# Three small loads requested from ScalarE's queue instead of GpSimd's, in a fused S4 convolution and linear-attention kernel

## The chip, the cores and the metric

The kernel runs on one core of a Trainium2 chip. The metric is the device time of one execution in microseconds (us). A core has five engines with an instruction queue each: TensorE (PE in the profile; its weight loads are PEld), VectorE (DVE), ScalarE (ACT), GpSimd (POOL) and SyncE (SP), which here only requests transfers. A transfer (DMA) is requested by an instruction in the queue of SyncE, ScalarE or GpSimd and is carried out by 16 DMA engines; the request itself occupies the queue of the engine that makes it (ACTq, SPq in the profile).

## What is computed

One input `A_u` of 2048 positions by 512 channels goes through two branches, which a gate mixes. Cut to what matters:

```
g = sigmoid(sum(x * gate_w))                      # one number per position
# branch a: state-space convolution
K = real(sum_n C * exp(dt * A * l) * dt * B)      # dt = exp(log_dt); 512 channels, 2048 taps, 128 states
a = causal convolution of x with K (reference: FFT of length 4096) + x * Dskip
# branch b: linear attention, 32 heads of 16
q, k, v = x @ wqkv
phi(t)  = [softmax(t @ w_phi), softmax(-(t @ w_phi))]
b = (phi(q) (phi(k)^T v) / (phi(q) sum phi(k))) @ wo
out = g * a + (1 - g) * b
```

The inputs are bfloat16. The three small ones in this case are `w_phi` (32 x 16 x 16, 16 KB), `gate_w` (512 numbers, 1 KB) and `Dskip` (512 numbers, 1 KB).

## The kernel before

The work is a list of small nodes (a few instructions each), with an engine, the data that each reads and writes, and an order. `Plan.add` and `Plan.dma` collect the nodes; `Plan.run` emits them in the order of the constant `ORDER`, two characters a node. Nothing is rescheduled when the program is built: within an engine the instructions stand in the order in which the nodes are emitted. Synchronisation between engines is put in by the framework, from the tiles that instructions read and write.

The stages overlap. First the tables and parameters are made (`prepare`, L197 on): sines and exponentials on ScalarE, their arguments on VectorE, index numbers (iota) on GpSimd. At the same time `wqkv` is loaded transposed and folded with `w_phi` on TensorE (`fold`, L519), which gives the weights of the keys (tile WW) and of the queries (Wqp). Then come keys and values (pk L699, vp L680), the convolution's Fourier stages and kernel generation (kps L182), the queries and the mix.

What stands at the start, queue by queue:

- SyncE asks for the six parameter matrices B_re, A_re, A_im, C_re, B_im, C_im (L216, 128 KB each, in this order), then for the transposed load of `wqkv` (L1506, lands in a part of tile Dtab), five transposed loads of x (L500, tile xT), two writes of a split parameter (L352, tile pz), a sixth xT, the value weights (L1509, tile WW) and sixteen pieces of x (L1496, tile UD).
- ScalarE asks for log_dt twice (L1491 as a column, tile ldc; L1492 spread over all partitions, tile ld), loads an activation table (L65), casts the index columns (L237, tile if), then takes exponentials of ld (L68, tile pt) and ldc (tile dtc), loads the table of sines and goes on with twelve sine and absolute-value instructions.
- GpSimd makes the iotas (L41, L46), asks for the three small loads (L1501 wc, L1502 gw, L1503 Dcol_b), then makes two masks (L468, L470), Wphi (L475, from wc and a mask: `w_phi` laid out block-diagonally), gwr (L488, from gw), some constants, two tiles for selE (L456, L458), Dcol and diagD (L482, L483, from Dcol_b) and a cleared tile (L785).
- TensorE transposes the parameters (psri, L372), and then folds (L519, reads Wphi and Dtab).

How a landing is signalled matters here. Each transfer that SyncE or ScalarE requests gets one of eight semaphores, in turn over both queues in the order of emission. A transfer whose semaphore an earlier one still holds waits, in the queue of the engine that requests it, until that earlier one has landed. Transfers that GpSimd requests have semaphores of their own. In the kernel before, the first eight holders are: 0 ldc, 1 B_re, 2 ld, 3 A_re, 4 A_im, 5 C_re, 6 B_im, 7 C_im; the next are the load of `wqkv` (0) and the xT loads (1 to 5).

The node of the small loads is `wsm` in `prepare`, its body `load_small` in `full_kernel`; `eng` of the node only tells the plan which engine's queue it stands in, and the call in the body decides which engine asks. The nodes that read its data name `wsm` among their keys (`at1` Wphi, `at2` diagD, `at3` gwr).

Of the kernel before, what the change touches and what calls it, by code (L numbers as in the profile page):

```python
# [10 lines left out]
ACT = mybir.ActivationFunctionType  # L11
# [186 lines left out]
def prepare(P, nc, g, evict, psum):  # L198
# [16 lines left out]
    for k, src in g.params:  # L215
        P.dma("par", 0.45, 2.5, lambda k=k, src=src: nc.sync.dma_start(out=g.rawd[k][:], in_=src.rearrange("(g p) n -> p g n", p=128)),  # L216
              rw=("", "r" + k), move=0.9)
    for tg in range(4):
        P.dma("ud", 2.0, 2.0, lambda tg=tg: g.load_ud(tg), rw=("", f"ud{tg}"), move=2.5, cnt=4)
    P.dma("wsm", 1.5, 2.0, lambda: g.load_small(), rw=("", "wsm"), move=0.6, cnt=3, eng="POOL")  # L220
    P.dma("wtr", 0.7, 2.0, lambda: g.load_wqk(), rw=("", "wqk"), move=5.0)
    P.dma("wv", 0.5, 2.0, lambda: g.load_wv(), rw=("", "wv"), move=1.7)

# [117 lines left out]
    for qi, (k, col) in enumerate((("Are", "dtc"), ("Aim", "dt2"))):  # L341
        v, h = 2 * qi, 2 * qi + 1
# [190 lines left out]
def keys_and_spectrum(P, nc, g, psum):  # L533
# [6 lines left out]
    def evict(name, get, deps, **kw):  # L540
        return P.add(("ACT", "DVE"), name, lambda: P.copy(*get()), deps, drop=["psum"], **kw)
    polar, sx, xt, kp = prepare(P, nc, g, evict, psum)

    g.XUn = {}
# [884 lines left out]
def full_kernel(tc, A_u, A_A_re, A_A_im, A_B_re, A_B_im, A_C_re, A_C_im, A_log_dt, A_Dskip,  # L1429
                B_x, B_wqkv, B_w_phi, B_wo, gate_w, out):  # L1430
    nc = tc.nc
# [5 lines left out]
    with ExitStack() as ctx:  # L1437
        g, fc, at = Bag(), Bag(), Bag()
        P = Plan(nc, {"XAu": 1, "UDp": 1, "xst": 3, "Ek": 2, "Zk": 2, "vr": 2, "vb": 2, "acc": 1, "r8": 3, "ax": 1, "nrm": 1, "E": 2, "cs": 4, "A": 1, "R": 2,
                      "KD": 1, "XA0": 1, "XK": 2, "Zr": 2, "XUX": 3, "ln": 8}, {"ps": 2, "p0": 2, "bk": 3, "acc": 1, "pf": 2})  # L1440
# [57 lines left out]

        def load_small():
            with nc.allow_non_contiguous_dma(reason="small"):  # L1500
                nc.gpsimd.dma_start(out=g.wc[:], in_=B_w_phi.rearrange("(m h) e f -> (h e) m f", h=8))  # L1501
                nc.gpsimd.dma_start(out=g.gw[:], in_=gate_w.rearrange("(kt p) -> p kt", p=128))  # L1502
                nc.gpsimd.dma_start(out=g.Dcol_b[:], in_=A_Dskip.rearrange("(kt p) -> p kt", p=128))  # L1503

        def load_wqk():
            nc.sync.dma_start_transpose(out=g.wT, in_=B_wqkv[:, 0:1024])  # L1506
# [17 lines left out]
        def stat_tile():  # L1524
            g.pz = dram.tile([2, 2, 512, 128], BF16, name="pz")
        g.load_ld, g.load_ud, g.load_small, g.load_wqk, g.load_wv, g.load_wo = load_ld, load_ud, load_small, load_wqk, load_wv, load_wo
        g.shift_tmp, g.shift_psum, g.stat_tile = shift_tmp, shift_psum, stat_tile
        g.fc, g.act, g.at, g.xT, g.psP, g.aq, g.persist = fc, act, at, xT, psP, aq, persist
# [101 lines left out]
```

## Time and profile before

| | us |
|---|---|
| median of 3 runs | 255.8 |
| lowest, highest | 254.76, 257.3 |
| the profiled execution's own time | 254.74 |
| its span, first to last instruction | 251.5 |
| VectorE busy | 227.2 |
| ScalarE busy | 215.3 |
| TensorE busy | 197.0 |
| GpSimd busy | 12.5 |

The profile is of one execution. Its times count from the start of the span; the 3.2 us between span and time lie around it. A timeline line gives the start, the duration, the engine, the line in the code, the operation with the tile written and the tiles read, and in brackets how long the engine had been idle before and what released it. A chain line gives start, duration and what the chain of work that ended last was doing then; a releaser is inferred from semaphore events.

### The profile page before, as it was taken

The numbers are of one execution on the slowest core, as the hardware profiler recorded it, in microseconds if no ns is written. First come the engines' busy times: TensorE is split into PE (matmuls) and PEld (weight loads), VectorE is DVE, ScalarE is ACT, GpSimd is POOL, SyncE is SP. The second block draws the span as 40 slices with busy tenths as digits, with TensorE's granted clock in tenths as the row PEclk, the third lists the DMA queues.
The fourth block names the chain that finished last, engine by engine and source line by source line (L and its number), as shares of the span: only waits on it lengthen the run. The fifth ranks groups of instructions, "written<-read, shape, count | busy, mean of one in ns | idle before, by whom it ended". The sixth has DMA issues, their size and how long they took to land.

```text
span 251.5 us, 9945 instructions
## 1 busy us (share of the span) xinstructions
PE 197.0 (78%) x4441; PEld 135.7 (54%) x4464; DVE 227.2 (90%) x306; ACT 215.3 (86%) x297; POOL 12.5 (5%) x24
## 2 busy tenths in 40 slices
PE   0447999999855677976889757999998998998940
PEld 0343356567544442552667535675776686786630
DVE  5899998989999997999999999999999999996341
ACT  2998799999999999999999999998999998663200
POOL 8730000000000000000000000000000000000000
PEclk9999999999599999995899999999999999999985
DMA  5999997100790699204001777214955599999784
GB/s 113 212 181 212 160 208 119 41 3 3 227 264 14 183 280 289 93 13 148 23 3 62 176 253 232 64 44 138 245 169 177 174 279 225 256 218 190 164 114 79
DMA packets 78170, 38.01 MB, mean 151 GB/s; under 512 B 57120, under 2 KB 73136, under 8 KB 78128
## 3 DMA queue, kind: packets, MB, share of 16 engines
q1 hardware_dynamic: 75504, 36.71, 60.1%
q10 hardware_dynamic: 2528, 0.66, 1.7%
q8 instruction: 34, 0.56, 1.0%
q0 software_dynamic: 96, 0.02, 0.1%
q14 instruction: 8, 0.07, 0.1%
HBM read 21.12 MB, written 13.11 MB: 136 GB/s over the span
## 4 chain that ended last, share of the span: by engine, by line
ACT 39%; PE 24%; DVE 17%; DMA 10%; issue 6%; SPq 1%; ACTq 0%; DVEq 0%
ACT cs L68 9%; DMA ZT<-Zd 4%; PE kps L182 4%; ACT L65 3%; ACT XAu L148 3%; PE vp L680 3%; ACT xst L148 3%; DMA WW<-in_B_wqkv_dram 3%; ACT XA L148 3%; ACT E L68 2%; ACT Ek L68 2%; PE psz L1266 2%; DMA ld<-in_A_log_dt_dram 2%; PE psy L824 2%; ACT trg L68 2%
## 5 line engine op out<-in xcount | busy, mean ns | idle before, releaser
L182 PEld LDWEIGHTS <-A 128*32 128x32 bf16 x1600 | 27.8, 161 | 6.4 <-issue 2.8
L182 PE MATMUL kps<-R,A 128*32 128x64 bf16 x1600 | 29.3, 229 | 2.5 <-ACT XA L148 0.8
L68 ACT ACTIVATE cs<-args 128x1024 bf16<-128x1024 f32 x32 | 30.8, 1059 | 0.3 <-PE args L1026 0.2
L1103 DVE TENSOR_TENSOR A<-Ctab,Dtab 128x2048 bf16<-128x2048 bf16 x16 | 19.5, 1218 | 0.7 <-PE kps L182 0.7
L1124 DVE TENSOR_TENSOR R<-E,cs 128x2048 bf16<-128x2048 bf16 x16 | 19.5, 1217 | 0.0
L1108 DVE TENSOR_TENSOR A<-Ctab,Dtab 128x2048 bf16<-128x2048 bf16 x16 | 19.5, 1216 | 0.0
L1120 DVE TENSOR_TENSOR R<-E,cs 128x2048 bf16<-128x2048 bf16 x16 | 19.5, 1216 | 0.0
L148 ACT CAST XK<-psB 128x1024 bf16<-128x1024 f32 (+1 forms) x17 | 16.6, 1005 | 2.4 <-PE psB L195 2.4
L68 ACT ACTIVATE E<-args 128x1024 bf16<-128x1024 f32 x16 | 17.1, 1066 | 1.4 <-PE args L1048 1.4
L68 ACT ACTIVATE Ek<-pk 128x512 bf16<-128x512 f32 x32 | 16.7, 598 | 1.1 <-PE pk L699 0.9
L699 PE MATMUL pk<-WW,xT 128*128 128x512 bf16 x57 | 15.4, 417 | 2.7 <-DVE Wqp L150 1.5
L68 ACT ACTIVATE Eq<-pq 128x512 bf16<-128x512 f32 (+1 forms) x28 | 16.8, 700 | 0.7 <-PE pq L843 0.7
L148 ACT CAST Zr<-psz 128x1024 bf16<-128x1024 f32 x15 | 15.8, 1051 | 1.4 <-PE psz L1266 1.4
L1234 DVE TENSOR_TENSOR t<-XUX,XK 128x2048 bf16<-128x2048 bf16 x14 | 16.8, 1215 | 0.0
L843 PE MATMUL pq<-xT,Wqp 128*128 128x512 bf16 x64 | 16.3, 396 | 0.0
L148 ACT CAST XA<-psA 128x1024 bf16<-128x1024 f32 (+1 forms) x15 | 14.8, 1018 | 1.5 <-DVE XA L150 1.5
L65 ACT ACT_TABLE_LOAD x11 | 14.1, 1283 | 2.1 <-issue 1.9
L1266 PE MATMUL psz<-t,TI 128*128 128x512 bf16 x49 | 14.7, 381 | 1.4 <-ACT xT L148 0.4
L189 PE MATMUL psA<-W,KD 128*64 128x128 bf16 x256 | 10.5, 227 | 5.7 <-ACT KD L148 3.1
L589 PE MATMUL psB<-XAu,TB 64*128 64x128 bf16 x256 | 11.0, 241 | 4.3 <-ACT xst L148 1.9
L726 DVE TENSOR_REDUCE Zk<-Ek 128x64 f32<-128x1024 bf16 x12 | 13.9, 1210 | 0.0
L189 PEld LDWEIGHTS <-KD 128*64 128x64 bf16 x256 | 8.4, 113 | 9.5 <-issue 4.9
(208 smaller groups left out, 475.4 us busy)
## 6 DMA issues: line engine op xcount, KB each, us to landing
XUX<-XUd SPq DMA_DIRECT2D x32, 256.0 KB
XUd<-xst SPq DMA_DIRECT2D x8, 512.0 KB
ax<-apd SPq DMA_DIRECT2D x16, 256.0 KB
Zd<-Zr SPq DMA_DIRECT2D x15, 256.0 KB
ZT<-Zd SPq DMA_DIRECT2D x13, 256.0 KB
UD<-in_A_u_dram SPq DMA_DIRECT2D x16, 128.0 KB
XUd<-xst SPq DMA_DIRECT2D x8, 256.0 KB
out_dram<-xT SPq DMA_DIRECT2D x8, 96.0 KB
```

Source lines behind the costliest of these rows:

```text
L65: return self.nc.scalar.preload_act_table_set(name)
L68: return self.nc.scalar.activation(**kw)
L148: self.nc.scalar.copy(out=o, in_=i)
L182: nc.tensor.matmul(kps[32 * dj:32 * dj + 32, g4, e, :], lhsT=A[:, ka, :, :, d].rearrange("p a b -> p (a b)"), rhs=R[:, kr, d, :], start=(i ...
L189: nc.tensor.matmul(ps[64 * ri:64 * ri + 64], lhsT=lhsT, rhs=fc.W1[:, ri].rearrange("p r d -> p (r d)"), start=True, stop=True, tile_positi ...
L843: nc.tensor.matmul(box.ps[:, m - m0, :] if late else box.ps[:], lhsT=g.Wqp[:, kt, 128 * m:128 * m + 128], rhs=xT[:, 4 * b:4 * b + 4, kt, : ...
L1103: nc.vector.tensor_tensor(out=c.A[:, 0:2].rearrange("p o a b c -> p (o a) b c"), in0=g.C[U // 8][:, 0:2, :, d0 % 256:d0 % 256 + 32].rearra ...
L1108: nc.vector.tensor_tensor(out=c.A[:, 2:4].rearrange("p o a b c -> p (o a) b c"), in0=g.C[U // 8][:, 1:3, :, d0 % 256:d0 % 256 + 32].rearra ...
L1120: nc.vector.tensor_tensor(out=c.R[:, :, :, 32:64], in0=t.E[:, 1].unsqueeze(1).to_broadcast([128, 2, 32, 32]), in1=t.cs[:], op=ALU.mult)
L1124: nc.vector.tensor_tensor(out=c.R[:, :, :, 0:32], in0=t.E[:, 0].unsqueeze(1).to_broadcast([128, 2, 32, 32]), in1=t.cs[:, ::-1, :, ::-1], o ...
L1234: nc.vector.tensor_tensor(out=box.t, in0=Ls[r0 // ns].X[:], in1=box.XK[:].unsqueeze(1).to_broadcast([128, 2, 1024]), op=ALU.mult)
L1266: nc.tensor.matmul(box.ps[:, hb, :], lhsT=fc.TI[:, k].rearrange("p t h a -> p (t h a)"), rhs=box.t[:, k, 512 * hb:512 * hb + 512], start=( ...
```

## The change

The node `wsm` is declared for ScalarE, and `load_small` calls ScalarE's queue:

```diff
-    P.dma("wsm", 1.5, 2.0, lambda: g.load_small(), rw=("", "wsm"), move=0.6, cnt=3, eng="POOL")
+    P.dma("wsm", 1.5, 2.0, lambda: g.load_small(), rw=("", "wsm"), move=0.6, cnt=3, eng="ACT")
...
         def load_small():
             with nc.allow_non_contiguous_dma(reason="small"):
-                nc.gpsimd.dma_start(out=g.wc[:], in_=B_w_phi.rearrange("(m h) e f -> (h e) m f", h=8))
-                nc.gpsimd.dma_start(out=g.gw[:], in_=gate_w.rearrange("(kt p) -> p kt", p=128))
-                nc.gpsimd.dma_start(out=g.Dcol_b[:], in_=A_Dskip.rearrange("(kt p) -> p kt", p=128))
+                nc.scalar.dma_start(out=g.wc[:], in_=B_w_phi.rearrange("(m h) e f -> (h e) m f", h=8))
+                nc.scalar.dma_start(out=g.gw[:], in_=gate_w.rearrange("(kt p) -> p kt", p=128))
+                nc.scalar.dma_start(out=g.Dcol_b[:], in_=A_Dskip.rearrange("(kt p) -> p kt", p=128))
```

`ORDER` is unchanged. In the built program the three requests leave GpSimd's queue (29 rows become 26) and stand in ScalarE's between the cast L237 and the exponential of ld (L68). They now take semaphores of the eight: the instruction order of ScalarE, with what each waits for, is

```
L65   LoadActFuncSet
L237  TensorCopy if<-ii             waits for VectorE
L1501 DMACopy wc<-in_B_w_phi_dram   waits for semaphore 1 (B_re landed)
L1502 DMACopy gw<-in_gate_w_dram    waits for semaphore 3 (A_re landed)
L1503 DMACopy Dcol_b<-in_A_Dskip    waits for semaphore 4 (A_im landed)
L68   Activation pt<-ld             waits for semaphore 2 (ld landed)
L68   Activation dtc<-ldc           waits for semaphore 0 (ldc landed)
```

On SyncE the order is the same, and the semaphores of the later transfers are shifted: the five xT loads wait for 2, 5, 6, 7 and 0 instead of 1 to 5, the two pz writes for 1 and 2 instead of 6 and 7, the sixth xT load for 3 (gw) instead of 0, WW for 4 (Dcol_b) instead of 1. On VectorE and TensorE no instruction moves.

## The prediction

> **What bounds the kernel now.** I read the page's busy shares and chain first, then the chain in order of time for the first 30 us, then the timelines of ScalarE, GpSimd, SyncE and TensorE over that stretch, and last its waits. The page says that no single engine bounds the whole, and that the chain that ended last is mostly engine work:
>
> ```profile
> PE 197.0 (78%) x4441; PEld 135.7 (54%) x4464; DVE 227.2 (90%) x306; ACT 215.3 (86%) x297; POOL 12.5 (5%) x24
> ACT 39%; PE 24%; DVE 17%; DMA 10%; issue 6%; SPq 1%; ACTq 0%; DVEq 0%
> ```
>
> GpSimd is 95% idle, and its last work of any weight ends at 15 us. So the change matters only through the start. There the chain in order of time (start, us, what) reads:
>
> ```profile
> 1.25 5.05 DMA ld<-in_A_log_dt_dram
> 6.30 0.02 issue
> 6.33 0.63 ACT pt L68
> 6.96 0.10 ACT dtc L68
> ...
> 12.84 0.95 ACT tgv L307
> 13.80 0.03 issue
> 13.82 1.71 DVE tgv L286
> ```
>
> The chain starts with ScalarE waiting for the load of log_dt, and then follows ScalarE without a gap to 13.8. Whatever makes ScalarE start later at 6.33 makes the whole start later. What surrounds that point is seen in the timelines (start, us, engine, line, work; in brackets the idle time before it and its releaser). ScalarE and its queue:
>
> ```profile
> 0.73 0.49 ACTq L1491 DMA_DIRECT2D ldc<-in_A_log_dt_dram  x1
> 1.25 0.59 ACTq L1492 DMA_DIRECT2D ld<-in_A_log_dt_dram  x1
> 1.88 1.28 ACT L65 ACT_TABLE_LOAD   x1 [1.88 <-issue]
> 3.17 0.20 ACT L237 CAST if<-ii 128x8 f32<-128x8 int32 x1
> 6.33 0.63 ACT L68 ACTIVATE pt<-ld 128x512 f32<-128x512 bf16 x1 [2.96 <-DMA ld<-in_A_log_dt_dram]
> ```
>
> GpSimd, SyncE and TensorE:
>
> ```profile
> 3.19 0.96 POOL L1501 DMA_DIRECT2D wc<-in_B_w_phi_dram  x1
> 3.44 1.16 SPq L216 DMA_DIRECT2D Cim<-in_A_C_im_dram  x1
> 4.15 0.77 POOL L1502 DMA_DIRECT2D gw<-in_gate_w_dram  x1
> 4.64 6.04 SPq L1506 DMA_TRANSPOSE Dtab<-in_B_wqkv_dram  x1
> 4.90 0.85 POOL L1503 DMA_DIRECT2D Dcol_b<-in_A_Dskip_dram  x1
> 6.73 0.34 PEld L372 LDWEIGHTS <-Are 128*128 128x128 bf16 x4 [6.73 <-DMA Are<-in_A_A_re_dram]
> 7.30 0.34 PEld L372 LDWEIGHTS <-Aim 128*128 128x128 bf16 x4 [0.23 <-DMA Aim<-in_A_A_im_dram]
> 8.41 1.50 POOL L475 TENSOR_TENSOR Wphi<-wc,mask 128x512 bf16<-128x512 bf16 x1 [1.74 <-DMA wc<-in_B_w_phi_dram]
> 13.05 0.77 PEld L519 LDWEIGHTS <-Dtab 128*128 128x128 bf16 x8 [2.76 <-DMA Dtab<-in_B_wqkv_dram]
> 27.23 2.98 PE L680 MATMUL vp<-WW,xT 128*128 128x512 bf16 x13 [0.36 <-DMA WW<-in_B_wqkv_dram]
> ```
>
> Two of the TensorE lines are used as clocks: A_re landed just before 6.73 and A_im just before 7.30, because TensorE stood waiting for them. The last line is the only place near the start where the chain has slack: TensorE had been ready 0.36 us before WW landed.
>
> **The change part by part.**
>
> *Taken from GpSimd.* Three requests, 0.96 + 0.77 + 0.85 = 2.58 us of its queue. Its next work, the masks (5.78 to 6.67), would start about 3.4, but Wphi waits for wc, not for the masks. Gain: 0. Wphi ended at 9.91, and its reader (L519) waited until 13.05 for the transposed Dtab, so even an earlier Wphi buys nothing.
>
> *Added to ScalarE: the requests themselves.* The nearest rows are ScalarE's own requests, 0.32 to 0.59 us (0.49 for ldc, which like gw and Dcol_b is four 2-byte elements on each of 128 partitions). Three are 3 x 0.49 = 1.47 us. ScalarE sits idle for 2.96 us between L237 and L68, so taken alone they would be hidden, and the forecast would be no change.
>
> *Added to ScalarE: waits.* This decides the case, and the diff does not show it. A load from SyncE or ScalarE signals its landing on one of eight semaphores in turn, and the ninth such load waits for the first to land, and so on. GpSimd's loads had semaphores of their own. In the built program of the changed kernel wc waits for B_re's semaphore, gw for A_re's, Dcol_b for A_im's. They stand in ScalarE's order after L237 and ahead of pt (L68). B_re is asked for before A_re, so wc is out by 6.73 at the latest. gw can't be asked for before 6.73, nor Dcol_b before 7.30. Then Dcol_b's request ends at 7.30 + 0.49 = 7.79, and with the 0.04 us that lay between request and next instruction after ld (1.84 to 1.88), pt starts at about 7.83, not 6.33: 1.50 us later. Bounds: with 0.32 us for a request (the shortest on ScalarE, at 241.9) 1.33 us; with 1.16 us each, the request of Cim, which SyncE made just ahead of the transposition, gw runs from 6.73 to 7.89, Dcol_b from 7.93 to 9.09, pt starts at 9.13, 2.80 us later. I take 1.50, since ScalarE's own rows are nearest.
>
> *Who waits behind it.* ScalarE's order from pt on has no gap until 22.9 us, so all of it moves: dtc, the table load, the sines, the second-buffer release for VectorE's tgv at 13.82, then ppx, PE's second L519 group at 16.78 (released by ppx), Wqp and WW, and pk at 22.05. pk ended at 26.87 (27.23 less 0.36) and now ends at 28.37. WW is asked for by SyncE, which waits for nothing of this and lands it near 27.2 as before, so vp starts at 28.37 and not 27.23: the delay is 1.50 - 0.36 = 1.14 us. With the bounds: 0.97 and 2.44.
>
> *SyncE's queue.* The three loads enter the rotation, so SyncE's waits move too: the first xT transposition waits for ld (6.30) instead of B_re, the fifth (issued after 16) for Dtab (13.05), the sixth for gw and WW for Dcol_b (both due before 13). All have landed by then; cost 0. The three loads as small packets: the 512 two-byte packets of ldc took about 8 ns each in the trace's packet records, so 1,536 of them are 1536 x 8 / 16 = 0.77 us on each of the 16 DMA engines, against 96 packets of GpSimd's queue at 2.0% of the first 12 us, 0.24 us. So Dtab and WW may land 0.5 us later: 13.6 and 27.7. Dtab is covered by ppx (16.8), WW by pk's new end of 28.37; without that cover WW's 0.5 would be on the path.
>
> *GpSimd's followers.* If wc lands 5.1 us after a request at 6.73 at worst, Wphi runs from 11.8 to 13.3, 0.3 us past the old start of L519, where TensorE then waits for ppx anyway. gw would land by 7.22 + 5.2 = 12.4, holding gwr and the rest of GpSimd's row up by 2.5 us; its first reader in a hurry is selE at 23.7, made from tiles ready at 12.9. Cost 0.
>
> *Sum.* The profiled execution took 254.7 us (span 251.5 and 3.2 around it): 254.7 + 1.1 = 255.9. It lies 1.1 below the median of the three runs, 255.8, so by the median the forecast is 255.8 + 1.1 = 256.9, say 257.0.
>
> *A rule against the trace.* The Trainium skill, DMA: Bandwidth & Descriptors, "Issuing engines are not separate DMA queues", says that asking from several engines saves only the sequencer's issue time, usually small. By that rule the sum would be 0 and the time 255.8, since 1.47 us fit into the idle 2.96. The rows agree about the issue time, but the rule leaves out what the queue waits for, 7.30 against 6.33.
>
> **The rivals.**
>
> *Slower: the transposition holds ScalarE's requests.* SyncE's L1506 is being issued from 4.64 to 10.68, 6.04 us for one request, and gw and Dcol_b are to go out inside it. If the two queues share what makes descriptors, gw goes out at 10.68, Dcol_b ends at 10.68 + 2 x 0.49 + 0.04 = 11.70, pt starts at 11.74, 5.41 later, and vp 5.05 later: 260.8. For it: Cim, just ahead of L1506, took 1.16 against 0.46 to 0.51 for the five loads before it. Against it: ldc beside Bre (0.49 and 0.46) and at the end ScalarE's output requests at 242 beside SyncE's (0.32 and 0.55) show no queueing. No row has a ScalarE request inside a transposition. It decides once pt starts past 9.25 (6.33 + 0.36 + 1% of 255.8). The Trainium skill, same page, "Queues, rings and completion order", says that SyncE and ScalarE each have a ring on every engine but no descriptor generator of their own, which speaks for this rival; no run here shows it yet.
>
> *Hidden after all.* The 1.1 us at 28 us is taken back later where an engine waits for something that did not move, that is for SyncE's requests: 255.8. For it: SyncE issues from 21.3 to 47 without regard to the start. Against it: from 30 to 60 us the waits name engines and no DMA, and the DMA pieces later in the chain (Zd, ZT after 197) hang on data that moves too.
>
> *Faster: GpSimd's traffic goes.* Its packets took 0.24 us per DMA engine in the first 12 us. If A_im lands earlier by all of that, pt still starts at 7.6, and the time is 256.7. To be faster, pt would have to start before 6.33, and A_im land before 5.8. I see nothing for that.
>
> **How the numbers follow.** Forecast (waits bite, requests are short to moderate): 0.64, at 257.0, its own range 256.8 to 258.3. Transposition rival 0.18 at 260.8. Hidden 0.15 at 255.8. A real gain 0.03. About 1%, 2.6 us, is what a measurement of this kernel can tell from no change (its three runs spread over 2.5). The range reaches from 255.3, the hidden case less a half of that spread's lower side, to 260.0, which leaves out most of the transposition rival. Slower by over 1% (above 258.4): that rival and a little of the forecast's upper end, 0.22. Faster 0.03. Within 1%: 0.75.
>
> **What would show it.** In ScalarE's timeline of the changed kernel: three requests after L237, the first by 6.7, the second not before A_re, the third not before A_im, and pt at about 7.8, right behind the third, where ScalarE's wait for ld was. Request lengths near 0.5 support the forecast; one that lasts until L1506 ends supports the rival. vp should start near 28.4 released by pk and no longer by WW. I am wrong if pt starts near 6.33, if the delay at vp is not about 1.1, or if it is 1.1 there and gone at the end.

## The result, and the profile after

The changed kernel takes 257.66 us (median of 19 runs, 255.21 to 262.45), the kernel before 255.32 beside it (19 runs, 254.22 to 258.25). The ratio is 1.0076, 95% interval 1.0047 to 1.0105: 1.94 us slower, between 1.2 and 2.7. The ratio compares the means of the fast executions, 18 of each kernel, and so differs from the ratio of the medians. The profiled execution took 256.0 us (span 253.4, before 251.5).

The page's busy shares and its shares of the chain, of the changed kernel:

```profile
PE 201.9 (80%) x4464; PEld 136.9 (54%) x4464; DVE 227.2 (90%) x306; ACT 215.6 (85%) x297; POOL 8.8 (3%) x21
PE 31%; ACT 27%; DVE 27%; DMA 7%; issue 7%; SPq 0%; ACTq 0%; DVEq 0%
```

VectorE and ScalarE did the same work in the same time, and GpSimd is 3.7 us less busy, which the end does not show. The difference is where things stand in time. The timeline of the changed kernel, ScalarE's and SyncE's requests with TensorE's weight loads as clocks (start, us, engine, line, work, and in brackets the idle time before it and its releaser):

```profile
3.58 0.38 ACTq L1501 DMA_DIRECT2D wc<-in_B_w_phi_dram  x1
5.78 5.63 SPq L1506 DMA_TRANSPOSE Dtab<-in_B_wqkv_dram  x1
6.54 0.38 ACTq L1502 DMA_DIRECT2D gw<-in_gate_w_dram  x1
6.57 0.34 PEld L372 LDWEIGHTS <-Are 128*128 128x128 bf16 x4 [6.57 <-DMA Are<-in_A_A_re_dram]
7.08 0.41 ACTq L1503 DMA_DIRECT2D Dcol_b<-in_A_Dskip_dram  x1
7.10 0.34 PEld L372 LDWEIGHTS <-Aim 128*128 128x128 bf16 x4 [0.20 <-DMA Aim<-in_A_A_im_dram]
7.54 0.63 ACT L68 ACTIVATE pt<-ld 128x512 f32<-128x512 bf16 x1 [4.17 <-DMA wc<-in_B_w_phi_dram]
```

gw is asked for 0.03 us ahead of TensorE's first use of A_re, Dcol_b 0.02 ahead of its first use of A_im: both fit the landings that TensorE waited for. pt follows the third request's end (7.49) by 0.05. Its bracket names wc, which is wrong: wc was asked for at 3.58, and what pt stands behind is the third request. Nor was ld late: in the packet records of the two traces the last of its 128 packets of 1 KB ended at 5.90 before and at 5.86 here. Two requests went out inside SyncE's L1506 (5.78 to 11.41), in 0.38 and 0.41 us.

From pt the delay goes to VectorE through the table of sines. The changed kernel's timeline of VectorE and GpSimd, and further on two rows of VectorE's that are used as marks below (XAu at 74 us, the last wide product at 243):

```profile
14.23 1.04 POOL L483 TENSOR_TENSOR diagD<-ident,Dcol 128x512 bf16<-128x512 bf16 x1
15.03 1.68 DVE L286 TENSOR_SCALAR tgv<-tgc,one 128x1024 int32<-128x1024 f32 x1 [0.48 <-ACT tgv L307]
15.21 0.95 POOL L785 MEMSET KVbd<- 128x1024 bf16 x1
...
74.25 1.21 DVE L150 CAST XAu<-psA 128x1024 bf16<-128x1024 f32 x1
...
242.88 1.21 DVE L1370 TENSOR_TENSOR xT<-psy,gT 128x1024 bf16<-128x1024 f32 x1
```

The same two marks in the kernel before:

```profile
73.11 1.22 DVE L150 CAST XAu<-psA 128x1024 bf16<-128x1024 f32 x1
...
240.62 1.21 DVE L1370 TENSOR_TENSOR xT<-psy,gT 128x1024 bf16<-128x1024 f32 x1
```

tgv is 15.03 - 13.82 = 1.21 us late, XAu 74.25 - 73.11 = 1.14, the last product 242.88 - 240.62 = 2.26. So there are two questions: is the first 1.1 us what was predicted, for the reason given; and does the second 1.1, behind 75 us, belong to the change?

### The profile page after: what moved, and what is told of

The parts are those of the page before. It is cut to its first block, busy times and chain, and to the rows that moved or that the text cites. A ratio compares the mean times of both kernels' runs of the same rounds, so it can differ in the third digit from the quotient of the medians.

```text
span 253.4 us, 9966 instructions
## 1 busy us (share of the span) xinstructions
PE 201.9 (80%) x4464; PEld 136.9 (54%) x4464; DVE 227.2 (90%) x306; ACT 215.6 (85%) x297; POOL 8.8 (3%) x21
## 4 chain that ended last, share of the span: by engine, by line
PE 31%; ACT 27%; DVE 27%; DMA 7%; issue 7%; SPq 0%; ACTq 0%; DVEq 0%
PE pk L699 6%; ACT cs L68 6%; DMA ZT<-Zd 4%; PE vp L680 4%; PE kps L182 4%; DVE A L1108 3%; DVE A L1103 3%; DVE R L1124 3%; DVE R L1120 3%; DVE t L1234 3%; ACT xst L148 3%; ACT L65 2%; ACT XAu L148 2%; ACT trg L68 2%; PE psA L564 2%
## 5 line engine op out<-in xcount | busy, mean ns | idle before, releaser
L68 ACT ACTIVATE cs<-args 128x1024 bf16<-128x1024 f32 x32 | 30.8, 1063 | 0.3 <-PE args L1026 0.2
L699 PE MATMUL pk<-WW,xT 128*128 128x512 bf16 x64 | 17.2, 421 | 1.5 <-DVE Wqp L150 1.5
L68 ACT ACTIVATE E<-args 128x1024 bf16<-128x1024 f32 x16 | 17.0, 1061 | 1.7 <-PE args L1048 1.5
L68 ACT ACTIVATE Ek<-pk 128x512 bf16<-128x512 f32 x32 | 16.7, 598 | 1.3 <-PE pk L699 1.2
L68 ACT ACTIVATE Eq<-pq 128x512 bf16<-128x512 f32 (+1 forms) x28 | 16.7, 694 | 0.7 <-PE pq L843 0.7
L1266 PE MATMUL psz<-t,TI 128*128 128x512 bf16 x60 | 15.5, 380 | 1.2 <-DVE t L1234 0.7
## 6 DMA issues: line engine op xcount, KB each, us to landing
XUX<-XUd SPq DMA_DIRECT2D x32, 256.0 KB
ax<-apd SPq DMA_DIRECT2D x16, 256.0 KB
Zd<-Zr SPq DMA_DIRECT2D x15, 256.0 KB
ZT<-Zd SPq DMA_DIRECT2D x13, 256.0 KB
XUd<-xst SPq DMA_DIRECT2D x8, 256.0 KB
```

What stands on the lines that cost most here:

```text
L68: return self.nc.scalar.activation(**kw)
L699: nc.tensor.matmul(box.ps[:], lhsT=xT[:, st, kt, :], rhs=g.WW[:, kt, :], start=(kt == 0), stop=(kt == 3))
```

## The experiments

The theory on trial: the requests cost nothing; the landings that they wait for on ScalarE hold pt up. Rivals: the requests on ScalarE's queue cost by themselves; the relief of GpSimd changes something. Each kernel's ratio is to the kernel before, timed beside it.

**1. One wait without any move (e1_wait_aim).** The kernel before, with a read of one column of A_im put ahead of pt:

```diff
-    S("p_e", lambda: act(out=Tt(4)[:], in_=g.ld_b[:], func=ACT.Exp), r="act ldb tmp", w="t4")
+    def p_e():
+        w = g.up.tile([128, 1], BF16, name="w_")
+        nc.scalar.copy(out=w[:], in_=g.rawd["Aim"][:, 3, 127:128])
+        act(out=Tt(4)[:], in_=g.ld_b[:], func=ACT.Exp)
+    S("p_e", p_e, r="act ldb tmp", w="t4")
```

> The kernel before, its three loads left on GpSimd, with one added ScalarE instruction ahead of pt (L68): a copy of one column of A_im, whose value nobody uses, so that ScalarE waits for A_im there and asks for nothing. Theory (the wait for the landings is what costs): pt starts near 7.5 instead of 6.33, vp near 28.1, and the time is 0.8 to 1.9 us above the kernel before, about as the changed kernel. Rival (the requests themselves, or their small packets, cost the time): within 0.3 us of before, since none is moved.

Measured: 256.30 us, ratio 1.0038 (1.0004 to 1.0072), so +0.97. ScalarE's timeline:

```profile
6.90 0.19 ACT L257 COPY w__185<-Aim 128x1 bf16<-128x1 bf16 x1 [3.53 <-DMA Aim<-in_A_A_im_dram]
7.00 0.62 ACT L68 ACTIVATE pt<-ld 128x512 f32<-128x512 bf16 x1
```

A wait for A_im alone makes the kernel slower, with all three requests still on GpSimd. pt is 0.67 late here and 1.21 in the changed kernel. The interval is 0.1 to 1.8 us, so the time alone only just speaks against the rival's 0.3.

**2. A later wait (e2_wait_cim).** The same with C_im, the last parameter to land.

> As the run with the wait for A_im, but ScalarE's added copy reads C_im, which landed at 9.0 in the trace of before: a longer dose of the same wait. Theory: pt starts near 9.2, 2.9 later; vp 2.5 later; the time 2.5 us above before if a delay at the start is carried to the end one to one, 3.5 or more if a later start also costs more in the later stages. Rival (later waits on SyncE's queue take a delay up): less than 1.5 us.

Measured: 258.09 us, ratio 1.011 (1.0068 to 1.0151), +2.8. The copy stood until 9.39, pt started at 9.49. pt is 3.16 behind the profile of before, VectorE's XAu only 2.21 (75.32): the missing 0.9 is that tgv took 0.81 us here in place of 1.71. That was not expected, and experiments 7 to 10 follow it up. The time fits the 2.5 us that were expected (the interval is 1.7 to 3.9) and rules out the rival's 1.5 or less; it does not tell 2.5 from 3.5.

**3. The requests behind pt (e3_late).** The changed kernel with the node of the small loads moved in `ORDER` behind pt, dtc and the table load:

```diff
-              "0W0y0B0K0h0i2U030M1f2C2D2E0L1e0l0f1I2I0C2F2G0R2L2M060N0X15...
+              "0W0B0K0h0i2U030M1f2C2D2E0L1e0l0f1I2I0C2F2G0R2L2M060N0y0X15...
```

> The changed kernel with the three requests moved back in ScalarE's queue, behind pt, dtc and the second table load. Their semaphores there belong to A_re, C_re and B_im, landed at 6.7, 7.7 and 8.1 in the trace of before. Theory: pt starts at 6.3 again, the third request ends near 8.5, the first sine starts at 8.4 to 8.6, and the time is within 0.4 us of before. Rival (requests cost ScalarE their own length, or their packets slow SyncE's queue): 0.8 us or more above before.

Measured: 254.16 us, ratio 0.9958 (0.9928 to 0.9989), 1.07 us *faster* than before, where a time within 0.4 us of before was expected. The three requests ran at 6.30, 7.24 and 7.66 (0.38, 0.38, 0.52 us), the first beside pt and the others under the table load (6.79 to 8.07); pt started at 6.05, when ld landed. The first sine started at 8.22, behind the third request's end at 8.18 and 0.15 behind the table load's: that is all that the requests cost ScalarE here. Where the gain comes from is not shown in full. ld landed 0.28 earlier than in the first profile of before, but the second one has pt at 6.02 too (experiment 5), so that is no gain of this edit; the short tgv is one:

```profile
13.68 0.82 DVE L286 TENSOR_SCALAR tgv<-tgc,one 128x1024 int32<-128x1024 f32 x1 [0.61 <-ACT tgv L307]
...
15.14 1.04 POOL L483 TENSOR_TENSOR diagD<-ident,Dcol 128x512 bf16<-128x512 bf16 x1
```

GpSimd's multiply for diagD, which in the kernels before and after begins ahead of tgv, begins here after it has ended.

**4. ld asked for ahead of ldc as well (e4_late_ldfirst).** Experiment 3 with ScalarE's first two requests exchanged.

> As the late requests, and in addition ld is asked for ahead of ldc on ScalarE's queue, so 0.5 us earlier. Theory (the start hangs on ld's landing once the waits are gone): ld lands 0.3 to 0.5 us earlier, pt starts near 5.9, and the time is 0.3 to 0.5 us below that of the late requests. Rival (ld's landing is set by the DMA engines and not by when it is asked for): no difference.

Measured: 255.63 us, ratio 1.0023 (0.999 to 1.0057). A miss. pt started at 4.75, but dtc, its neighbour, then waited 0.91 us for ldc, until 6.29, so that only 0.29 us of the lead were left. The first sine lost them and more, at 8.59 against 8.22 in experiment 3:

```profile
8.59 1.06 ACT L68 ACTIVATE TB<-tgv 128x1024 bf16<-128x1024 int16 x1 [0.80 <-DVE pt L345]
```

The table load had ended at 7.79. The third request ended at 8.55, after the parameters had landed later in this execution (A_re's first use at 6.64, 6.32 in experiment 3), and the sine followed it by 0.04, as it did there. The releaser in the bracket can't be right: in experiment 3 the sine started while that same VectorE instruction was still running (8.03 to 8.72). So the waits of the requests held ScalarE up here too, by 0.8 us, at a later place.

**5. and 6. A second profile of each kernel (e5_before_again, e6_after_again).** No edit.

> The kernel before, unchanged, for a second profiled execution. If the extra 1.1 us that the changed kernel's profile shows behind the 75th microsecond is only variation of TensorE's half-clock stretches from execution to execution, the half-clock total here differs from the first profile's 13.65 us by several us (20 or more), and VectorE's last instructions shift by up to 1 us or more against the first profile, while the shift up to 75 us stays within 0.5 us. If the extra belongs to the change, the total is again about 13.7 us and the span 251.5.

> The kernel after, unchanged, for a second profiled execution. Theory of the waits: the exponentials' first activation again starts 0.0 to 0.1 us behind the third request's end, and VectorE is 0.9 to 1.4 us behind the first profile of before until 75 us; behind that the shift follows the half-clock total. Rival, that the extra 1.1 us behind 75 us belongs to the change: the same 2.2 to 2.3 us at the end as in the first profile of after.

Measured: before 255.01 (span 252.1), after 257.74 (span 255.2). In the second profile of before pt starts at 6.02 instead of 6.33, because ld landed earlier. XAu stands at 72.78, the last product at 241.62: 0.33 earlier than in the first profile at 73 us and 1.00 later at the end. In the second profile of after pt starts at 7.51, XAu at 74.21 and the last product at 244.08: the same as the first at 74 us and 1.20 later at the end. So the same program gains or loses 1.2 to 1.3 us behind 75 us from one execution to the next. The granted clock of TensorE (the page's PEclk row, in 40 slices of 6.3 us) of before, first profile:

```profile
PEclk9999999999599999995899999999999999999985
```

of before, second profile:

```profile
PEclk9999999999576997995699999999999999999985
```

and of after, first profile:

```profile
PEclk9999999999578999996599999999999999999985
```

The first profile of before has the fewest slices below 9: by the table of windows its clock is 0.83 from 60 to 80 us and 0.86 from 110 to 135, against 0.66 and 0.80 in the second profile of the same kernel and 0.74 and 0.80 in after's first. From 80 to 110 us it was 1.00 and 0.94 in the two profiles of before; after's second profile has 0.74, 0.89 and 0.93 in the three stretches, its first 1.00 in the middle one. Counted as time at half clock (a stretch at 0.83 has 2 x 0.17 of its length there), that is about 14 and 27 us for before, as far apart as was expected, but 20 and 20 for after, whose two profiles still end 1.2 us apart. So the end does not follow this total alone, as had been expected, and what moves it is open. The second 1.1 us can't be put down to the change, since one program varies by as much; nor are they excluded, for the second pair of profiles has 1.03 there (2.46 at the end, 1.43 at XAu).

**7. GpSimd's work held (e7_hold).** Is GpSimd what makes tgv long? The kernel before, with a tiny read ahead of diagD that waits until ScalarE has written the second half of TJ, behind tgv:

```diff
+        z = wp.tile([128, 1], BF16, name="z_")
+        e.tensor_copy(out=z[:], in_=fc.TJ[:, 63, 31:32])
         e.tensor_copy(out=Dcol[:], in_=g.Dcol_b[:])
```

> The kernel before with the work that GpSimd does beside VectorE's second tgv (diagD's multiply and KVbd's fill) held until ScalarE has written the second half of TJ; no request is moved. Collision theory: tgv takes about 0.81 us in place of 1.71, VectorE is about 0.9 us earlier from 15 to 75 us, and the time is 0.6 to 1.0 us below before (ratio 0.996 to 0.998). Rival, that the late variant gained because the requests left GpSimd's queue: tgv may be short here too, but VectorE gains nothing downstream and the time is that of before within 0.3 us. Third reading, that held work is late for somebody else: the stage behind needs diagD or KVbd, and the gain is given back before 40 us.

Measured: 255.80 us, ratio 1.0016 (0.9979 to 1.0053). The timeline of GpSimd and VectorE:

```profile
13.23 0.81 DVE L286 TENSOR_SCALAR tgv<-tgc,one 128x1024 int32<-128x1024 f32 x1 [0.47 <-ACT tgv L307]
...
17.08 2.60 DVE L312 TENSOR_SCALAR TB<-TB 64x2048 bf16<-64x2048 bf16 x2
17.48 0.95 POOL L787 MEMSET KVbd<- 128x1024 bf16 x1
```

The gain was lost before 40 us, as the third reading had it, but not for its reason. tgv is short, but the held work, diagD (16.50 to 17.54) and the fill of KVbd (17.48 to 18.43), now meets L312, which takes 2.60 us against 1.38 in the kernel before. 0.9 us won, 1.2 lost.

**8. The same hold on the changed kernel (e8_after_hold).**

> The changed kernel with the same hold on GpSimd. Theory (waits and collision are separate terms that add): the first activation of the exponentials still starts at about 7.5 us, tgv takes 0.81 in place of 1.68, VectorE is 0.2 to 0.4 us behind before from 15 to 75 us, and the time is 0.8 to 1.0 us below the changed kernel, 0.3 to 1.1 above before. Rival, that one delay hides the other: the time stays at the changed kernel's, 1.9 us above before.

Measured: 256.78 us, ratio 1.0075 (1.0045 to 1.0105), the ratio of the changed kernel; the gain of 0.8 to 1.0 us that was expected is not there. tgv 0.81, L312 2.60 again: what the hold wins at one place it loses at the next.

**9. A shorter hold (e9_hold_half).** Experiment 7 with the wait on the first half of TJ, so that diagD and KVbd fall between the two:

```diff
-        e.tensor_copy(out=z[:], in_=fc.TJ[:, 63, 31:32])
+        e.tensor_copy(out=z[:], in_=fc.TJ[:, 0, 0:1])
```

> The kernel before with GpSimd's diagD and KVbd held only until ScalarE has written the first half of TJ, so that they lie between VectorE's second tgv and its trigonometric rows at L312. Collision theory: tgv 0.81 us (before 1.71) and the two instructions of L312 1.38 us together (2.60 under the longer hold), VectorE 0.9 us earlier than before at 15 us and still 0.9 earlier at 36 to 75 us (plus or minus 0.3 for the landing of ld), and the time 0.6 to 1.0 us below before, ratio 0.996 to 0.998. Rival, that VectorE's early stage is not what the end waits for: the shift is there at 15 us and gone by 36 us, and the time is that of before within 0.3 us.

Measured: the trace did as expected, the time did not show it. tgv 0.81, and L312 in one go:

```profile
15.87 0.95 POOL L787 MEMSET KVbd<- 128x1024 bf16 x1
17.37 1.38 DVE L312 TENSOR_SCALAR TB<-TB 64x2048 bf16<-64x2048 bf16 x2
```

XAu stands at 71.92, 1.19 earlier than in the first profile of before and 0.86 earlier than in the second. But the median is 255.72 us, ratio 1.0003 (0.997 to 1.0035), outside the 0.996 to 0.998 that was expected, though the interval reaches into it. In the profile itself the last wide product starts at 241.91, 0.29 later than in the second profile of before: there the lead was gone by the end.

**10. The shorter hold on the changed kernel (e10_after_hold_half).**

> The changed kernel with the same shorter hold. Theory, that the waits of the requests and the collision are separate and add: the exponentials' first activation at 7.5 to 7.8 us as in the changed kernel, tgv 0.81 (1.68), L312 1.38, VectorE 0.2 to 0.5 us behind before from 36 to 75 us, and the time 0.6 to 1.0 us below the changed kernel, so 0.9 to 1.3 above before, ratio 1.003 to 1.005. Rival, that the stage behind takes the gain: ratio 1.007 to 1.008 again.

Measured: 256.05 us, ratio 1.002 (0.9984 to 1.0057). pt at 7.42, tgv 0.81, L312 1.38, XAu at 73.44. The interval holds the expected 1.003 to 1.005 and leaves out the rival's 1.007 to 1.008, but it holds 1 as well, and experiment 9 found no gain from the same hold. In the traces the two terms are separate: with the meeting gone from both kernels (this one and experiment 9) pt is 1.39 later and XAu 1.52. That they add in time is not shown.

**11. The first request alone (e11_wc_only).** The changed kernel with gw and Dcol_b back on GpSimd:

```diff
-                nc.scalar.dma_start(out=g.gw[:], in_=gate_w.rearrange("(kt p) -> p kt", p=128))
-                nc.scalar.dma_start(out=g.Dcol_b[:], in_=A_Dskip.rearrange("(kt p) -> p kt", p=128))
+                nc.gpsimd.dma_start(out=g.gw[:], in_=gate_w.rearrange("(kt p) -> p kt", p=128))
+                nc.gpsimd.dma_start(out=g.Dcol_b[:], in_=A_Dskip.rearrange("(kt p) -> p kt", p=128))
```

> The change cut to its first request: only wc is asked for by ScalarE, gw and Dcol_b stay on GpSimd. Theory of the waits: wc's request waits for B_re alone, which lands at 3.5 us, goes out at 3.5 to 3.6 and is over by 4.0, two us before ld lands, so the exponentials' first activation starts with ld's landing (5.7 to 6.4 us), VectorE stands within -0.6 and +0.1 of before up to 75 us, and the time is that of before within 0.6 us (ratio 0.998 to 1.002). Rival, that the requests on ScalarE's queue cost by being there, or that GpSimd's relief does it: a third or more of the whole change's 1.9 us, ratio 1.0025 or more, or a gain of 0.6 us and more.

Measured: 255.92 us, ratio 1.0003 (0.9964 to 1.0043). ScalarE's timeline:

```profile
3.52 0.40 ACTq L1501 DMA_DIRECT2D wc<-in_B_w_phi_dram  x1
...
5.80 0.63 ACT L68 ACTIVATE pt<-ld 128x512 f32<-128x512 bf16 x1 [2.43 <-DMA ld<-in_A_log_dt_dram]
```

A request that waits for an early landing fits into ScalarE's idle time: pt started with ld's landing. The time shows no cost, but its interval (-0.9 to +1.1 us) also holds the rival's 1.0025; against it speaks the trace.

**12. The first two requests (e12_wc_gw).** The changed kernel with Dcol_b's request back on GpSimd.

> The change cut to its first two requests: wc and gw on ScalarE, Dcol_b on GpSimd. Theory of the waits: gw's request waits for A_re and starts at 6.4 to 6.6 us, so the exponentials' first activation starts at 6.9 to 7.1 us, 0.5 us ahead of the whole change and 0.6 to 1.0 behind the landing of ld; VectorE 0.5 to 0.8 us behind the first profile of before from 15 to 75 us, time 0.7 to 1.4 us above before (ratio 1.003 to 1.0055). Rival, that the third request's wait for A_im alone does it all: ratio within 0.001 of 1.

Measured: 255.86 us, ratio 1.002 (0.9987 to 1.0053), below the 1.003 to 1.0055 that was expected; the interval holds that and the rival's 1 as well, so the time decides nothing here. ScalarE's timeline:

```profile
6.52 0.38 ACTq L1502 DMA_DIRECT2D gw<-in_gate_w_dram  x1
6.95 0.63 ACT L68 ACTIVATE pt<-ld 128x512 f32<-128x512 bf16 x1 [3.58 <-DMA wc<-in_B_w_phi_dram]
```

pt stands 0.05 behind the end of gw's request (the bracket names wc, wrongly again), 0.59 ahead of where the third request puts it. VectorE was not late at 15 us: gw landed so late that diagD began at 14.63, behind tgv's start at 14.44. tgv took 0.81, and this time diagD was the longer one, 1.52 us in place of 1.04. XAu at 73.45 is 0.34 behind the first profile of before; the loss that brings it there lies between 31 and 43 us and was not pursued.

## Why the prediction was right, and where it was not

The two kernels of the case and those of the experiments, in their order (pt and XAu: start in us; tgv: duration of the second one; ratio to before):

| kernel | pt | tgv | XAu | ratio |
|---|---|---|---|---|
| before, two profiles | 6.33, 6.02 | 1.71, 1.76 | 73.11, 72.78 | 1 |
| after, two profiles | 7.54, 7.51 | 1.68, 1.68 | 74.25, 74.21 | 1.0076 |
| wait for A_im | 7.00 | 1.71 | 73.83 | 1.0038 |
| wait for C_im | 9.49 | 0.81 | 75.32 | 1.011 |
| late | 6.05 | 0.82 | 72.08 | 0.9958 |
| late, ld first | 4.75 | 0.81 | 72.71 | 1.0023 |
| hold | 5.74 | 0.81 | 72.78 | 1.0016 |
| after, hold | 7.82 | 0.81 | 75.10 | 1.0075 |
| short hold | 6.03 | 0.81 | 71.92 | 1.0003 |
| after, short hold | 7.42 | 0.81 | 73.44 | 1.002 |
| wc only | 5.80 | 2.05 | 73.06 | 1.0003 |
| wc and gw | 6.95 | 0.81 | 73.45 | 1.002 |

Against the mean of before's two profiles (72.95), the lateness of XAu gives the measured difference in time within 0.7 us in nine of the eleven other kernels. The two that stand out are late with ld first (0.24 early, 0.6 slower) and the short hold (1.03 early, 0.1 slower).

*The waits decide: right.* gw went out with A_re's landing, Dcol_b with A_im's, pt behind it. Experiment 1 brings half of the loss with the wait alone, 11 none of it with a request whose wait is over early, 12 places pt behind gw, and 3 takes the loss away with all three requests still on ScalarE. In all five executions where pt stands behind a request, it starts 0.04 to 0.05 us after that request's end.

*pt 1.50 us later, from requests of 0.49: right in the sum.* The requests took 0.38 to 0.41, the landings came 0.16 and 0.20 earlier, so pt was at 7.54 and not 7.83. But ld's landing in the profile of before, 6.30, was a late one: in the six executions in which pt waits for ld behind ldc (before twice, late, hold, short hold, wc only) pt starts at 6.00 on average, in the four with all three requests ahead of it (after twice and its two holds) at 7.57. The delay is 1.21 in the first pair of profiles and 1.57 on average.

*The slack of 0.36 at WW, taken off to 1.14: wrong.* This is the step that made the forecast too small. I followed the chain of waits through vp, where TensorE had waited 0.36 us for WW. In the changed kernel vp does follow pk without that wait, at 28.11 and not 28.37, 0.88 late; but VectorE does not hang on vp there. From 16 to 38 us its timeline shows no wait, and it carries the whole delay past that point (pt, L383, from 30.51 to 31.68). Zk in the kernel before, and in the changed one:

```profile
26.00 4.59 DVE L726 TENSOR_REDUCE Zk<-Ek 128x64 f32<-128x1024 bf16 x4
27.18 4.59 DVE L726 TENSOR_REDUCE Zk<-Ek 128x64 f32<-128x1024 bf16 x4
```

The slack itself was an accident of one profile. In the second profile of before vp follows pk without a wait for WW, at 26.62, and in the second of after it starts at 28.17, 1.55 later. So the delay of about 1.1 at vp, named as a sign, reads 0.88 in one pair and 1.55 in the other. In experiment 11 pk ended at 24.84, 2.03 us earlier than in the first profile of before, TensorE then waited 1.72 us for WW, and XAu still stood at 73.06 (73.11 before):

```profile
26.56 5.35 PE L680 MATMUL vp<-WW,xT 128*128 128x512 bf16 x24 [1.72 <-DMA WW<-in_B_wqkv_dram]
```

Between the second profiles, pt is 7.51 - 6.02 = 1.49 late and XAu 74.21 - 72.78 = 1.43; between the first, 1.21 and 1.14. Here two engines were both full, and slack on one of them was no slack of the kernel. That the first pair gave just the 1.14 that I had named was luck: a delay 0.29 smaller, and a deduction of 0.36 that VectorE did not get. The start of the sum was off too: 255.8 was the median of three executions, the nineteen beside the changed kernel have 255.32. So 257.0 came within 0.7 us of the measured 257.66 with 0.5 us from a start that was too high; the difference itself was forecast at 1.1 and measured at 1.94. Without the deduction it would have been 1.5. What is left, 1.94 against 1.5, lies inside the interval of 1.2 to 2.7, and I leave it open.

*GpSimd's 2.58 us saves 0: right in result, not for the whole reason.* I looked only at who waits for GpSimd's results. GpSimd's place in time has a price of its own, the meeting of diagD and KVbd with tgv, about 0.9 us in tgv. In the changed kernel it stayed, because gw's late landing (gwr waited for it until 11.56) kept GpSimd's row as late as VectorE's. In all six executions with a long tgv (before and after twice each, wait for A_im, wc only) tgv ends 0.54 to 0.55 us behind the end of KVbd's fill. So at 16 us VectorE's delay of 1.2 hung on GpSimd's row, held up by gw, as much as on ScalarE's; that ScalarE's alone is enough is seen in the pair of short holds.

*The transposition rival: dead.* Requests of 0.38 and 0.41 us inside L1506. By the same rows the rule that was weighed (the Trainium skill, DMA: Bandwidth & Descriptors, "Issuing engines are not separate DMA queues") is right about the requests' own time and gives the wrong time here, 255.8, since it says nothing of what stands queued behind a request that waits.

*Hidden after all: no.* 1.14 of the 1.21 us at pt are there at 74 us, and the timed runs show 1.2 or more at the end.

*SyncE's and the packets' terms: covered, as said.* Dtab landed at 13.88, in the second profile at 13.56 (13.05 and 12.99 before, 13.6 forecast), ppx released that stage at 17.96; pk ended at 28.27, and vp did not wait for WW.

*What stays open.* Whether the 0.9 to 1.2 us by which the short hold is ahead at 72 us are worth time: 1.0003 (0.997 to 1.0035) says hardly, the late variant's 0.9958 (0.9928 to 0.9989) with the same XAu says yes, and the two intervals overlap. The late variant is the only version here that is measurably below the kernel before.

## What to carry to other kernels

Before a request is moved to another engine's queue, look up which semaphore it will take and when that semaphore's last holder lands: the request's own 0.4 us may be free, but here the engine stood until that landing, and everything behind it in its order stood too. Take slack off a delay only if every full engine passes through the place where the slack is, and only if a second profile has it; look at the gap-free engine rather than at the chain of waits alone. And look at two profiles of the kernel before: here ld's landing varied by 0.6 us (pt 5.74 to 6.33), half of the effect.

## What the runs showed of the hardware that was not expected

VectorE and GpSimd held each other up. The second tgv took 0.81 us alone or where it started first, and 1.68 to 2.05 where diagD had started ahead of it and KVbd followed; the two instructions of L312 took 1.38, and 2.60 with the end of diagD and the fill of KVbd beside them; dt (128 x 4) took 0.17 before and 0.98 in the changed kernel beside Wphi. The other way round, diagD took 1.52 in place of 1.04 where tgv had started first (experiment 12). The Trainium skill, SBUF — State Buffer, "Who interferes with whom", says that the two engines share a pair of ports, that tensor_scalar can take it in a mode that uses two ports, and that whoever issues first blocks the other for the whole instruction. The traces agree: L312 lost 1.22 of the 1.35 us in which GpSimd was still at work beside it (17.08 to 18.43 in experiment 7), the long tgv always ended 0.54 to 0.55 behind KVbd's end, and diagD and KVbd, which had started first, took their 1.04 and 0.95 as elsewhere. That the port is the cause no run here shows by itself.

The stretches at half clock fall differently in each execution of one program: in before's two profiles the clock was 0.83 and 0.66 from 60 to 80 us. The Trainium skill, TensorE: Matmul & The Clock Gate, "What's actually happening", says that the gate judges TensorE's activity over windows that run freely and do not start with the kernel; the two profiles are in line with that. That the 1.2 to 1.3 us between executions behind 75 us come from it is not shown: the two profiles of after have a mean granted clock of 0.944 and 0.941 and still end 1.2 us apart.
